# State times weights, formed per batch, ahead of the first layer: a cross-attention with a maxout FFN on one core

## The chip, the cores and the metric

The kernel runs on one core of a Trainium2 chip. The time is that of one execution on the device, in microseconds (us). The core has a matrix engine (TensorE, "PE" in the profile, with its weight loads as "PEld"), three engines for elementwise work (VectorE "DVE", ScalarE "ACT", GpSimd "POOL") and SyncE ("SP"), which here only issues transfers. Matmuls write to PSUM, a small memory of eight banks of 2 KB for each of 128 partitions; VectorE and ScalarE empty it into SBUF. Each engine takes its instructions in order and waits on semaphores for the others.

## The reference

There are 8 batches of 8 heads. Per head, 512 rows of x and 32 rows of state, 64 numbers each, read one another by attention. The results of all heads stand side by side as rows of 512, 544 per batch, 4352 in all, and go through a feed-forward layer with a maximum over three products.

```python
# x (8, 8, 512, 64), state (8, 8, 32, 64); w1, w2, w3 (512, 768); w_out (768, 512)
a      = softmax(x @ state^T / 8)        # 512 x 32 per head
xread  = a @ state                       # 512 x 64 per head
a2     = softmax(state @ x^T / 8)        # 32 x 512 per head
sread  = a2 @ x                          # 32 x 64 per head
X      = rows of [xread; sread], heads side by side       # 4352 x 512
h      = maximum(X @ w1, X @ w2, X @ w3)                  # 4352 x 768
out    = h @ w_out                                        # 4352 x 512, float32
```

## The kernel before

All inputs are loaded by GpSimd's queue, which turns float32 into bfloat16 on the way: the state (L65), eight transfers for a block-diagonal copy of it (bd_sb, L73), x in 32 transfers of 128 rows by all heads (x_sb, L85), the three weights (L90) and w_out (L93). The state's transposes go through PSUM and 64 small ScalarE copies into stateT_bd (L107, L109), where two heads stand in diagonal blocks.

Attention runs over the batches, and in each over four chunks of 128 rows. A chunk is transposed head pair by head pair (pxt, by the helper at L48), copied by ScalarE (xT, L139), multiplied with stateT_bd (ps, L143) and exponentiated (e_b, L151). VectorE sums over the 32 states (den, L157), takes the reciprocal (L160) and multiplies (a_sb, L162); a_sb is transposed (pat, L48) and copied (aT_b, L176). Then, for each of four head pairs, one matmul on 64 rows of the array forms xread, transposed (pxr, L184), which ScalarE copies into AT (L191); eight matmuls form sread and the column sums (psr, L195, L203), and VectorE divides (L211, L212, L216). pxr and psr have one PSUM buffer each.

AT holds all 4352 rows, transposed, in 4 x 128 partitions. The feed-forward stage runs over tiles of 512 rows, eight and a half of them. For each of six blocks m of 128 columns of h there are three times four matmuls of 512 columns (pw, L240); ScalarE copies the first product (L249), VectorE takes the two maxima (L250, L251) into ht. Six times four matmuls form the output of a tile (po, L256), ScalarE copies (L264) and SP stores (L265).

The order on each engine is made by a scheduler that fills free engines with what is ready; that is why transposes of the next chunk stand between the matmuls of the last one. The two stages open their own PSUM pools, so that only a little of the feed-forward runs before attention ends.

Of the kernel before, what the change touches and what calls it, by code (L numbers as in the profile page):

```python
# [15 lines left out]
def kernel(  # L17
# [9 lines left out]
):  # L27
    nc = tc.nc
# [7 lines left out]
    assert HD == d_model  # L36
    assert out.shape[0] == T and out.shape[1] == d_model

    NSC = S // 128
    NKT = HD // 128  # L40
    NMT = d_ff // 128
    NKO = d_ff // 128
    NHP = H // 2

    scale = 1.0 / (D ** 0.5)

    def tr(out_ap, in_ap, ident_ap, *, start, stop, tile_position=(0, 0)):
        nc.tensor.matmul(out_ap, in_ap, ident_ap,  # L48
                         is_transpose=True, start=start, stop=stop,
                         tile_position=tile_position)  # L50

    const = ctx.enter_context(tc.tile_pool(name="const", bufs=1))
    ident = const.tile([128, 128], BF16)
    make_identity(nc, ident)
    ones128 = const.tile([128, 128], BF16)
    nc.gpsimd.memset(ones128, 1.0)

    inpool = ctx.enter_context(tc.tile_pool(name="in", bufs=1))
    atpool = ctx.enter_context(tc.tile_pool(name="at", bufs=1))
    wpool = ctx.enter_context(tc.tile_pool(name="weights", bufs=1))  # L60

    AT = atpool.tile([128, NKT, T], BF16)

    state_sb = inpool.tile([32, B, H, D], BF16)
    nc.gpsimd.dma_start(out=state_sb, in_=state.rearrange("b h n d -> n b h d"))  # L65

    bd_sb = inpool.tile([128, B, 2, 128], BF16)
    nc.gpsimd.memset(bd_sb, 0.0)
    for hq in range(2):
        for hp4 in range(4):  # L70
            h = hq * 4 + hp4
            c0 = (h % 2) * 64
            nc.gpsimd.dma_start(  # L73
                out=bd_sb[hp4 * 32:(hp4 + 1) * 32, :, hq, c0:c0 + 64],
                in_=state[:, h, :, :].rearrange("b n d -> n b d"),
            )

    stateT_bd = inpool.tile([128, B, NHP, 2 * Ns], BF16)
    nc.gpsimd.memset(stateT_bd, 0.0)

    x_sb = inpool.tile([128, B, NSC, H, D], BF16)
    xr = x.rearrange("b h (sc p) d -> p b sc h d", p=128)
    for b in range(B):
        for sc in range(NSC):
            nc.gpsimd.dma_start(out=x_sb[:, b, sc, :, :], in_=xr[:, b, sc, :, :])  # L85

    w_sb = []
    for i, w in enumerate([moe_w1, moe_w2, moe_w3]):
        wt = wpool.tile([128, NKT, d_ff], BF16, name=f"w{i}")
        nc.gpsimd.dma_start(out=wt, in_=w.rearrange("(kk p) f -> p kk f", p=128))  # L90
        w_sb.append(wt)
    wout_sb = wpool.tile([128, NKO, d_model], BF16, name="wout")
    nc.gpsimd.dma_start(out=wout_sb,  # L93
                        in_=moe_w_out.rearrange("(kk p) f -> p kk f", p=128))

    with tc.tile_pool(name="psum_st", bufs=2, space=bass.MemoryType.PSUM) as pst:
        for b in range(B):
            pt = pst.tile([128, NHP, Ns], BF16)
            for hp in range(NHP):
                tr(  # L100
                    pt[:, hp, :],
                    state_sb[:, b, 2 * hp:2 * hp + 2, :],
                    ident[:Ns, :Ns],
                    start=(hp == 0), stop=(hp == NHP - 1),
                )
            for hp in range(NHP):
                nc.scalar.copy(out=stateT_bd[0:64, b, hp, 0:Ns],  # L107
                               in_=pt[0:64, hp, :])
                nc.scalar.copy(out=stateT_bd[64:128, b, hp, Ns:2 * Ns],  # L109
                               in_=pt[64:128, hp, :])  # L110

    xTpool = ctx.enter_context(tc.tile_pool(name="xT", bufs=3))
    epool = ctx.enter_context(tc.tile_pool(name="e", bufs=2))
    apool = ctx.enter_context(tc.tile_pool(name="a", bufs=3))
    aTpool = ctx.enter_context(tc.tile_pool(name="aT", bufs=2))
    redpool = ctx.enter_context(tc.tile_pool(name="red", bufs=6))

    with (
        tc.tile_pool(name="p_xT", bufs=2, space=bass.MemoryType.PSUM) as p_xT,
        tc.tile_pool(name="p_S", bufs=2, space=bass.MemoryType.PSUM) as p_S,  # L120
        tc.tile_pool(name="p_aT", bufs=2, space=bass.MemoryType.PSUM) as p_aT,
        tc.tile_pool(name="p_xr", bufs=1, space=bass.MemoryType.PSUM) as p_xr,
        tc.tile_pool(name="p_sr", bufs=1, space=bass.MemoryType.PSUM) as p_sr,
    ):
        for b in range(B):
            e_b = epool.tile([128, NSC, H, Ns], BF16, tag="e")
            aT_b = aTpool.tile([128, 2, NSC, 128], BF16, tag="aT")

            for sc in range(NSC):
                pxt = p_xT.tile([128, NKT, 128], BF16, tag="pxt")  # L130
                for hp in range(NHP):
                    tr(
                        pxt[:, hp, :],
                        x_sb[:, b, sc, 2 * hp:2 * hp + 2, :],
                        ident,
                        start=(hp == 0), stop=(hp == NHP - 1),
                    )
                xT = xTpool.tile([128, NKT, 128], BF16, tag="xT")
                nc.scalar.copy(out=xT, in_=pxt)  # L139

                ps = p_S.tile([128, NHP, 2 * Ns], F32, tag="pS")
                for hp in range(NHP):
                    nc.tensor.matmul(  # L143
                        ps[:, hp, :],
                        xT[:, hp, :],
                        stateT_bd[:, b, hp, :],
                        start=(hp == 0), stop=(hp == NHP - 1),
                        tile_position=(0, 0),
                    )

                nc.scalar.activation(  # L151
                    out=e_b[:, sc, :, :],
                    in_=ps.rearrange("p hp (q n) -> p hp q n", q=2),
                    func=AF.Exp, scale=scale,
                )
                den = redpool.tile([128, H], F32, tag="den")
                nc.vector.reduce_sum(out=den, in_=e_b[:, sc, :, :], axis=AX.X)  # L157
                rden = redpool.tile([128, H], BF16, tag="rden")
                with nc.allow_low_precision("softmax denom reciprocal"):
                    nc.vector.reciprocal(out=rden, in_=den)  # L160
                a_sb = apool.tile([128, H, Ns], BF16, tag="a")
                nc.vector.tensor_mul(  # L162
                    out=a_sb,
                    in0=e_b[:, sc, :, :],
                    in1=rden.unsqueeze(2).to_broadcast((128, H, Ns)),
                )

                pat = p_aT.tile([128, 2, 128], BF16, tag="pat")
                for hqq in range(2):
                    tr(  # L170
                        pat[:, hqq, :],
                        a_sb[:, 4 * hqq:4 * hqq + 4, :],
                        ident,
                        start=(hqq == 0), stop=(hqq == 1),
                    )
                nc.vector.tensor_copy(out=aT_b[:, :, sc, :], in_=pat)  # L176

            for hp in range(NHP):
                h0 = 2 * hp
                hq = h0 // 4  # L180
                p0 = (h0 % 4) * 32

                pxr = p_xr.tile([128, S], F32, tag="pxr")
                nc.tensor.matmul(  # L184
                    pxr,
                    bd_sb[p0:p0 + 64, b, hq, :],
                    aT_b[p0:p0 + 64, hq, :, :],
                    start=True, stop=True,
                    tile_position=(p0, 0),
                )  # L190
                nc.scalar.copy(out=AT[:, hp, b * SP:b * SP + S], in_=pxr)  # L191

                psr = p_sr.tile([128, 2, 2 * Ns], F32, tag="psr")
                for sc in range(NSC):
                    nc.tensor.matmul(  # L195
                        psr[:, 0, :],
                        x_sb[:, b, sc, h0:h0 + 2, :],
                        e_b[:, sc, h0:h0 + 2, :],
                        start=(sc == 0), stop=False,
                        tile_position=(0, 0),  # L200
                    )
                for sc in range(NSC):
                    nc.tensor.matmul(  # L203
                        psr[:, 1, :],
                        ones128,
                        e_b[:, sc, h0:h0 + 2, :],
                        start=False, stop=(sc == NSC - 1),
                        tile_position=(0, 0),
                    )
# [87 lines left out]
```

## Time and profile before

| | |
|---|---|
| runs | 278.49, 281.87, 282.01 us; median 281.87 us |
| profiled execution, first to last instruction | 279.6 us |
| mean granted TensorE clock in it | 0.896 of full |
| TensorE, first layer (L240) | 648 matmuls, 135.7 us busy |
| TensorE, second layer (L256) | 204 matmuls, 45.5 us busy |
| ScalarE's copies into AT (L191) | 32, 18.7 us busy; idle 29.5 us before them, for pxr |
| data read and written in memory | 15.73 MB and 8.91 MB |

The list of runs gives no time of its own for the profiled execution; its span stands in its place. Busy times of matmuls overlap with one another, since the engine is pipelined: 648 matmuls of the first layer last 370 ns each on average in the profile but start some 210 ns apart. So for TensorE it is better to read starts, or the chain of waits, than sums of durations. The granted clock is a share of full speed; it has two values in this trace, 1.00 and 0.50.

### The profile page before, as it was taken

The numbers are of one execution on the slowest core, as the hardware profiler recorded it, in microseconds if no ns is written. First come the engines' busy times: TensorE is split into PE (matmuls) and PEld (weight loads), VectorE is DVE, ScalarE is ACT, GpSimd is POOL, SyncE is SP. The second block draws the span as 40 slices with busy tenths as digits, with TensorE's granted clock in tenths as the row PEclk, the third lists the DMA queues.
The fourth block names the chain that finished last, engine by engine and source line by source line (L and its number), as shares of the span: only waits on it lengthen the run. The fifth ranks groups of instructions, "written<-read, shape, count | busy, mean of one in ns | idle before, by whom it ended". The sixth has DMA issues, their size and how long they took to land.

```text
span 279.6 us, 3945 instructions
## 1 busy us (share of the span) xinstructions
PE 239.7 (86%) x1492; PEld 122.7 (44%) x1492; DVE 131.9 (47%) x332; ACT 108.2 (39%) x249; POOL 41.1 (15%) x54
## 2 busy tenths in 40 slices
PE   0128878778776699999999999999999999999993
PEld 0017546535432344444444444444444444444581
DVE  0007897777877664334235235235135145145160
ACT  0989965645553132222322331331331332322321
POOL 9999990000000000000000000000000000000000
PEclk9999995555555589999999999999999999999999
DMA  5999999910000000120120120110210210210211
GB/s 38 59 144 149 154 155 204 208 25 0 2 1 2 0 1 0 43 109 0 58 94 0 73 77 2 76 75 0 76 77 0 79 74 0 96 56 2 109 41 75
DMA packets 44801, 17.01 MB, mean 61 GB/s; under 512 B 38128, under 2 KB 40432, under 8 KB 44784
## 3 DMA queue, kind: packets, MB, share of 16 engines
q0 software_dynamic: 39888, 7.87, 33.1%
q1 hardware_dynamic: 4896, 8.92, 8.3%
q8 instruction: 11, 0.18, 0.3%
q14 instruction: 6, 0.05, 0.1%
HBM read 15.73 MB, written 8.91 MB: 88 GB/s over the span
## 4 chain that ended last, share of the span: by engine, by line
PE 77%; POOL 12%; ACT 5%; DVE 3%; DMA 1%; issue 1%; ACTq 0%; POOLq 0%
PE pw L240 48%; PE po L256 16%; POOL x_sb L85 8%; PE pxr L184 5%; ACT AT L191 3%; PE psr L195 2%; PE pxt L48 2%; POOL bd_sb L73 2%; PE psr L203 2%; DMA x_sb<-in_x_dram 1%; PE ps L143 1%; PE pat L48 1%; ACT e_b L151 1%; DVE rd L211 1%; DVE a_sb L162 1%
## 5 line engine op out<-in xcount | busy, mean ns | idle before, releaser
L240 PE MATMUL pw<-AT,w 128*128 128x512 bf16 (+1 forms) x648 | 135.7, 370 | 0.0
L240 PEld LDWEIGHTS <-w 128*128 128x128 bf16 x648 | 63.3, 98 | 69.3 <-issue 1.6
L250 DVE TENSOR_TENSOR tmpm<-tmpm,pw 128x512 f32<-128x512 f32 (+1 forms) x54 | 35.5, 657 | 96.4 <-PE pw L240 91.0
L249 ACT COPY tmpm<-pw 128x512 f32<-128x512 f32 (+1 forms) x54 | 30.3, 562 | 87.1 <-PE pw L240 87.1
L256 PE MATMUL po<-wout,ht 128*128 128x512 bf16 x204 | 45.5, 379 | 0.0
L251 DVE TENSOR_TENSOR ht<-tmpm,pw 128x512 bf16<-128x512 f32 (+1 forms) x54 | 35.5, 658 | 5.7
L264 ACT COPY o_sb<-po 128x512 f32<-128x512 f32 x34 | 19.9, 586 | 39.0 <-PE po L256 39.0
L256 PEld LDWEIGHTS <-ht 128*128 128x128 bf16 x204 | 20.0, 98 | 23.9 <-DVE ht L251 1.6
L191 ACT CAST AT<-pxr 128x512 bf16<-128x512 f32 x32 | 18.7, 585 | 29.5 <-PE pxr L184 29.5
L85 POOL DMA_DIRECT2D x_sb<-in_x_dram x32 | 28.0, 1022 | 0.0
L184 PE MATMUL pxr<-aT_b,bd_sb 64*128 64x512 bf16 x32 | 16.9, 528 | 8.6 <-ACT AT L191 8.1
L211 DVE RECIPROCAL rd<-psr 128x64 f32<-128x64 f32 x32 | 17.8, 555 | 12.7 <-PE psr L203 11.8
L157 DVE TENSOR_REDUCE den<-e_b 128x8 f32<-128x256 bf16 x32 | 12.6, 412 | 22.6 <-ACT e_b L151 22.4
L48 PE MATMUL pxt<-ident,x_sb 128*128 128x128 bf16 x128 | 19.0, 277 | 3.8 <-ACT stateT_bd L109 2.8
L139 ACT COPY xT<-pxt 128x512 bf16<-128x512 bf16 x32 | 18.2, 594 | 3.2 <-PE pxt L48 3.1
L195 PEld LDWEIGHTS <-x_sb 128*128 128x128 bf16 x128 | 8.3, 119 | 22.0 <-DVE den L157 8.9
L48 PE MATMUL pt<-ident,state_sb 32*128 32x32 bf16 x32 | 2.0, 183 | 15.4 <-ACT stateT_bd L109 9.2
L143 PE MATMUL ps<-stateT_bd,xT 128*128 128x64 bf16 x128 | 11.5, 228 | 3.9 <-ACT e_b L151 2.6
L48 PE MATMUL pat<-ident,a_sb 128*128 128x128 bf16 x64 | 12.1, 288 | 3.0 <-DVE a_sb L162 3.0
L48 PEld LDWEIGHTS <-x_sb 128*128 128x128 bf16 x128 | 11.9, 127 | 5.0 <-issue 4.9
L162 DVE TENSOR_TENSOR a_sb<-e_b,rden 128x256 bf16<-128x256 bf16 x32 | 13.4, 422 | 0.5
L195 PE MATMUL psr<-e_b,x_sb 128*128 128x64 bf16 x128 | 12.6, 229 | 1.0 <-DVE AT L216 0.9
(27 smaller groups left out, 102.2 us busy)
## 6 DMA issues: line engine op xcount, KB each, us to landing
out_dram<-o_sb SPq DMA_DIRECT2D x34, 256.0 KB, 2.0
x_sb<-in_x_dram POOLq DMA_DIRECT2D x32, 128.0 KB, 4.9
w<-in_moe_w_dram POOLq DMA_DIRECT2D x3, 768.0 KB, 12.4
wout<-in_moe_w_out_dram POOLq DMA_DIRECT2D x1, 768.0 KB, 18.7
state_sb<-in_state_dram POOLq DMA_DIRECT2D x1, 256.0 KB, 4.6
bd_sb<-in_state_dram POOLq DMA_DIRECT2D x8, 32.0 KB, 2.3
```

What stands on the lines that cost most here:

```text
L48: nc.tensor.matmul(out_ap, in_ap, ident_ap, is_transpose=True, start=start, stop=stop, tile_position=tile_position)
L85: nc.gpsimd.dma_start(out=x_sb[:, b, sc, :, :], in_=xr[:, b, sc, :, :])
L184: nc.tensor.matmul(pxr, bd_sb[p0:p0 + 64, b, hq, :], aT_b[p0:p0 + 64, hq, :, :], start=True, stop=True, tile_position=(p0, 0),)
L191: nc.scalar.copy(out=AT[:, hp, b * SP:b * SP + S], in_=pxr)
L195: nc.tensor.matmul(psr[:, 0, :], x_sb[:, b, sc, h0:h0 + 2, :], e_b[:, sc, h0:h0 + 2, :], start=(sc == 0), stop=False, tile_position=(0, 0),)
L211: nc.vector.reciprocal(out=rd, in_=psr[:, 1, :])
L240: nc.tensor.matmul(pw[i][:, :nn], w_sb[i][:, kk, m * 128:(m + 1) * 128], AT[:, kk, n0:n0 + nn], start=(kk == 0), stop=(kk == NKT - 1), til ...
L249: nc.scalar.copy(out=tmpm[:, :nn], in_=pw[0][:, :nn])
L250: nc.vector.tensor_max(tmpm2[:, :nn], tmpm[:, :nn], pw[1][:, :nn])
L251: nc.vector.tensor_max(ht[:, m, :nn], tmpm2[:, :nn], pw[2][:, :nn])
L256: nc.tensor.matmul(po, ht[:, kt, j * 128:(j + 1) * 128], wout_sb[:, kt, :], start=(kt == 0), stop=(kt == NKO - 1), tile_position=(0, 0),)
L264: nc.scalar.copy(out=o_sb, in_=po)
```

## The change

The kernel is written anew around one identity. xread is a times state, per head; the first layer multiplies it with w. So for one batch, xread @ [w1 w2 w3] = a @ G, where G is state @ [w1 w2 w3], head by head: 256 rows (8 heads x 32 states) by 2304 columns. G is formed per batch in six pieces (`g_piece`) of eight matmuls each, with 64 rows and 32 columns of the array in use by each, and copied to SBUF by ScalarE. The first layer then contracts over 256, in two steps instead of four, and xread is never formed. The rows of sread still go through the weights, all 256 together at the end (`s_maxout`).

Other parts change with it. x is loaded with four neighbouring rows per partition, in eight transfers; the weights come in halves by column. Work of attention is done for a whole batch at once: `xt_piece` (16 transposes, two VectorE copies), `score_piece` (16 matmuls, one exponential of 1024 columns, a sum, a reciprocal, and the product with it on GpSimd), `sread_piece` (32 matmuls of 32 columns and 8 of 128, each on half of the array's columns) and `at_piece` (8 transposes, one copy). The order on the engines is the order of the code. The loop over batches has six slots; in slot m block m of the first layer of batch b is followed by parts of other batches: the second layer of b - 1, attention of b + 2, G of b + 1. All of these parts take their PSUM from one pair of two-bank buffers (tag "two"); the first layer has the other four banks (tag "pw").

```diff
+    ctx.enter_context(tc.manual_schedule())
...
+    load_x(0)
+    load_w(0)
+    load_w(1)
+    load_x(1)
+    load_x(2)
+    nc.gpsimd.dma_start(out=wout_sb, in_=moe_w_out.rearrange("(kk p) f -> p kk f", p=128))
+    for b in range(3, B):
+        load_x(b)
...
+    for g in range(2):
+        pt = pp.tile([128, 2048], BF16, tag="two", name="pt")
+        for t in range(8):
+            nc.tensor.transpose(
+                pt[:, 128 * t:128 * t + 128],
+                st_sb[:, 8 * g + t].rearrange("p c d -> p (c d)"), ident)
...
+    def xt_piece(b):
...
+        pxt = pp.tile([128, H, 2, 128], BF16, tag="two", name="pxt")
...
+            nc.vector.tensor_copy(out=xT[b][:, 4 * g:4 * g + 4], in_=pxt[:, 4 * g:4 * g + 4])
+
+    def score_piece(b):
+        ps = pp.tile([128, J, H, Ns], F32, tag="two", name="ps")
...
+        nc.scalar.activation(out=e[b], in_=ps, func=AF.Exp, scale=scale)
...
+        nc.vector.reduce_sum(out=den, in_=e[b], axis=AX.X)
...
+        nc.vector.reciprocal(out=rden, in_=den)
...
+        nc.gpsimd.tensor_mul(
+            out=a[b].rearrange("p j h n -> p (j h) n"),
...
+    def sread_piece(b):
+        psr = pp.tile([128, 1024], F32, tag="two", name="psr")
+        for j in range(J):
+            for h in range(H):
+                r, hh = h % 2, h // 2
+                nc.tensor.matmul(
+                    psr[64 * r:64 * r + 64, hh * Ns:hh * Ns + Ns],
+                    x_sb[b][:, h, j, :], e[b][:, j, slot(h), :],
+                    start=(j == 0 and hh == 0), stop=(j == J - 1), skip_group_check=True,
+                    tile_position=(0, 64 * r))
...
+    def at_piece(b):
+        pat = pp.tile([128, 2048], BF16, tag="two", name="pat")
...
+        nc.vector.tensor_copy(out=aT[b].rearrange("p q t -> p (q t)"), in_=pat[:, 0:1024])
...
+    def g_piece(b, u):
...
+        c, k = divmod(u, 3)
+        pg = pp.tile([128, 2, 512], F32, tag="two", name="pg")
+        for hh in range(NHP):
+            for r in range(2):
+                h = 2 * hh + r
+                nc.tensor.matmul(
+                    pg[32 * hh:32 * hh + 32, r, 0:384],
+                    bd[64 * r:64 * r + 64, b, h, r, :],
+                    w_sb[c][64 * r:64 * r + 64, hh, k * 384:(k + 1) * 384],
+                    start=True, stop=True, tile_position=(64 * r, 32 * hh))
+        nc.scalar.copy(out=G[b][:, :, u * 384:(u + 1) * 384], in_=pg[:, :, 0:384])
...
+    def maxout(b, m, n, lhs, rhs, nk):
...
+        for i in range(3):
+            p = pp.tile([128, 512], F32, tag="pw", bufs=4, name=f"pw{i}")
+            for k in range(nk):
+                nc.tensor.matmul(p[:, 0:n], lhs(i, m, k), rhs(k), start=(k == 0), stop=(k == nk - 1))
...
+        nc.scalar.copy(out=t0[:, 0:n], in_=pw[0][:, 0:n])
+        nc.vector.tensor_max(t1[:, 0:n], t0[:, 0:n], pw[1][:, 0:n])
+        nc.vector.tensor_max(ht[b][:, m, :], t1[:, 0:n], pw[2][:, 0:n])
...
+    def ffn_out(b, jj):
+        po = pp.tile([128, 2, d_model], F32, tag="two", name="po")
...
+        o = work.tile([128, 2, d_model], F32, tag="osb", bufs=3, name="osb")
+        nc.scalar.copy(out=o, in_=po)
...
+    for f in attention(0):
+        f()
+    for u in range(NG):
+        g_piece(0, u)
+    for f in attention(1):
+        f()
+
     for b in range(B):
...
+        slots = [[] for _ in range(NM)]
+        if b > 0:
+            slots[1].append(lambda: ffn_out(b - 1, 0))
+            slots[3].append(lambda: ffn_out(b - 1, 1))
+        if b + 2 < B:
+            for f, m in zip(attention(b + 2), (0, 2, 4, 5)):
+                slots[m].append(f)
+        if b + 1 < B:
+            for u in range(NG):
+                slots[u].append(lambda u=u: g_piece(b + 1, u))
+        for m in range(NM):
+            x_maxout(b, m)
+            for f in slots[m]:
+                f()
+    for m in range(NM):
+        s_maxout(m)
+        if m in (1, 3):
+            ffn_out(B - 1, m // 2)
+    ffn_out("s", 0)
```

GpSimd's queue before, its end (x_sb is x, w and wout are the weights). Its last rows are loads, with nothing behind them.

```order
L85 DMA x_sb<-in_x_dram 128x8x64 [waits DMASW0_49]
L90 DMA w_122<-in_moe_w_dram 128x4x768 [waits DMASW1_49]
L90 DMA w_124<-in_moe_w_dram 128x4x768 [waits DMASW2_49]
L90 DMA w_126<-in_moe_w_dram 128x4x768 [waits DMASW3_49]
L93 DMA wout<-in_moe_w_out_dram 128x6x512 [waits DMASW4_49]
L292 UNCONDITIONAL_BRANCH
```

GpSimd's queue after, from the weights on (w_88 and w_89 are their halves, x_81 to x_87 batches 1 to 7, a the normalized scores). The wait in brackets names one of eight semaphores of the loads, taken in turn.

```order
L81 DMA w_88<-in_moe_w_dram 128x4x384 x3
L81 DMA w_89<-in_moe_w_dram 128x4x384 x2
L81 DMA w_89<-in_moe_w_dram 128x4x384 [waits DMASW0_49]
L71 DMA x_81<-in_x_dram 128x8x256 [waits DMASW1_49]
L71 DMA x_82<-in_x_dram 128x8x256 [waits DMASW2_49]
L91 DMA wout<-in_moe_w_out_dram 128x6x512 [waits DMASW3_49]
L71 DMA x_83<-in_x_dram 128x8x256 [waits DMASW4_49]
L71 DMA x_84<-in_x_dram 128x8x256 [waits DMASW5_49]
L71 DMA x_85<-in_x_dram 128x8x256 [waits DMASW6_49]
L71 DMA x_86<-in_x_dram 128x8x256 [waits DMASW7_49]
L71 DMA x_87<-in_x_dram 128x8x256 [waits DMASW0_49]
L147 TENSOR_TENSOR a<-e,rden 128x1024 [waits DVE_49,Activation_49] x8
```

The weights moved ahead of all but the first batch of x, and the eight products that make a, which VectorE computed before, stand behind the last load.

ScalarE's queue before, in the middle of attention (AT is the transposed xread, e_b the exponentials, xT the transposed x):

```order
L191 CAST AT<-pxr 128x512 x4
L151 ACTIVATE e_b<-ps 128x256 x3
L139 COPY xT<-pxt 128x512
L151 ACTIVATE e_b<-ps 128x256
L139 COPY xT<-pxt 128x512 x3
```

ScalarE's queue after, in the loop, slots 1 to 3 of batch 1 (t is the copy of the first product, osb the output, G the piece of state times weights):

```order
L216 CAST t_699<-pw_690 128x512
L241 COPY osb<-po 128x1024
L202 CAST G<-pg 128x2x384
L216 CAST t_739<-pw_730 128x512
L141 ACTIVATE e<-ps 128x1024
L202 CAST G<-pg 128x2x384
L216 CAST t_788<-pw_779 128x512
```

The copies into AT and of xT are gone from ScalarE; a copy of G follows each copy of a first product, and the exponential and the output copies stand between the two.

More of the change, by code (lines that the diff above doesn't have):

```diff
@@ L65 @@
[L65 to L72, printed above, removed]
+    data = ctx.enter_context(tc.tile_pool(name="data", bufs=1))
+    wpool = ctx.enter_context(tc.tile_pool(name="weights", bufs=1))
+    work = ctx.enter_context(tc.tile_pool(name="work", bufs=2))
+    pp = ctx.enter_context(tc.tile_pool(name="pp", bufs=2, space=bass.MemoryType.PSUM))
@@ L93 @@
[L93 to L209, printed above, removed]
-                rd = redpool.tile([128, 2 * Ns], F32, tag="rd")
-                nc.vector.reciprocal(out=rd, in_=psr[:, 1, :])
-                nc.vector.tensor_mul(
-                    out=AT[0:64, hp, b * SP + S:b * SP + SP],
-                    in0=psr[0:64, 0, 0:Ns], in1=rd[0:64, 0:Ns],
-                )
-                nc.vector.tensor_mul(
-                    out=AT[64:128, hp, b * SP + S:b * SP + SP],
-                    in0=psr[64:128, 0, Ns:2 * Ns], in1=rd[64:128, Ns:2 * Ns],
-                )
@@ L270 @@
+    for m in range(NM):
+        s_maxout(m)
+        if m in (1, 3):
+            ffn_out(B - 1, m // 2)
+    ffn_out("s", 0)
 _INS = ['x', 'state', 'moe_w1', 'moe_w2', 'moe_w3', 'moe_w_out']
```

187 lines of the change are left out of this document (112 added, 75 removed).

## The prediction

> **What bounds the kernel now.** I read the page first (busy shares, the slices with the granted clock), then the chain that ended last, then stretches of the span, then the order of time on TensorE, last the groups of each engine by shape.
>
> ```profile
> span 279.6 us, 3945 instructions
> PE 239.7 (86%) x1492; PEld 122.7 (44%) x1492; DVE 131.9 (47%) x332; ACT 108.2 (39%) x249; POOL 41.1 (15%) x54
> PEclk9999995555555589999999999999999999999999
> 101.05 13.60 PE pw L240 x63
> 119.83 15.54 PE pw L240 x72
> 135.37 5.18 PE po L256 x24
> 264.87 7.86 PE pw L240 x72
> 272.73 2.60 PE po L256 x12
> 275.36 0.58 ACT o_sb L264
> ```
>
> There are two stages. From 101.05 us on the chain is TensorE alone: 72 matmuls of 512 columns take 15.54 us, 215.8 ns each, at full clock, and the same holds for the second layer (24 in 5.18 us). That stage is 174.3 us long and has no gap. The 101 us ahead of it are attention, over half of them at half clock:
>
> ```profile
> 26.00:38.00 12.00, 10.36 (x145) 7.13 (x142) 10.57 (x41) 10.39 (x24) 12.00 (x15) 1.00 2.37 151
> 38.00:42.00 4.00, 2.37 (x27) 1.22 (x27) 3.52 (x14) 2.62 (x6) 3.78 (x5) 0.95 2.15 159
> 42.00:95.00 53.00, 39.38 (x365) 23.99 (x363) 40.89 (x152) 25.23 (x54) 0.00 (x0) 0.50 0.33 58
> 42.00:49.00 7.00, 5.83 (x64) 4.33 (x62) 5.24 (x19) 3.81 (x9) 0.00 (x0) 0.50 1.16 203
> 30.27 0.37 PE L184 MATMUL pxr<-aT_b,bd_sb 64*128 64x512 bf16 x1 [0.29 <-ACT AT L191]
> 30.58 0.29 PE L195 MATMUL psr<-e_b,x_sb 128*128 128x64 bf16 x4
> 30.70 0.28 PE L203 MATMUL psr<-e_b,ones 128*128 128x64 bf16 x4
> 30.82 0.28 PE L48 MATMUL pat<-ident,a_sb 128*128 128x128 bf16 x2
> 30.93 0.28 PE L143 MATMUL ps<-stateT_bd,xT 128*128 128x64 bf16 x4
> 40.54 0.37 PE L184 MATMUL pxr<-aT_b,bd_sb 64*128 64x512 bf16 x1 [0.67 <-ACT AT L191]
> 42.84 0.40 PE L195 MATMUL psr<-e_b,x_sb 128*128 128x64 bf16 x4
> 43.06 0.40 PE L203 MATMUL psr<-e_b,ones 128*128 128x64 bf16 x4
> ```
>
> The columns after the length of a stretch are busy time and instructions of TensorE, weight loads, VectorE, ScalarE and GpSimd, then granted clock, DMA share and GB/s (as written to SBUF). In the rows in order of time the reader is to see start against start, not durations, which overlap. At full clock four matmuls of 64 columns take 0.12 us, 30 ns each, weight load included; a transpose of 128 columns takes 55 ns (two from 30.82 to 30.93). At half clock the same four take 0.22 us. A matmul on 64 rows of the array (pxr) holds the next one off for 0.31 us where its 512 columns need 0.216: a change between parts of the array and the whole costs about 0.095 us. And the clock fell at 42 with TensorE 2.37 us busy in the 4 us before and no gap over 0.67 us.
>
> **The change, part by part.** The first layer's contraction goes from four steps to two. A batch then needs 36 matmuls of 512 columns, not 72, and saves 36 x 0.2158 = 7.77 us; eight batches save 62.2 us. The state rows' part (72 of 256 columns, 7.86 us) and the second layer (5.18 us a batch, 2.60 us for the state rows) stay.
>
> What it adds is G: 48 matmuls a batch, each 64 rows by 32 columns of the array with 384 columns streamed. No row of before shows two such matmuls side by side. Their own columns take 384/512 x 215.8 = 162 ns. If the eight of a piece ran one behind the other, a piece would take 8 x 0.162 = 1.30 us; if they overlap and only issue parts them, 0.162 + 7 x 0.030 = 0.37 us. Below the first nothing but 0.162 us itself is possible. I take 0.37: the eight positions are disjoint and fill the array exactly once, each pair of row halves writes two different banks, and the row nearest to a 32-column piece is the small matmuls' 30 ns. [...]
>
> Attention of a batch is now 16 + 8 + 8 instructions of 128 columns and 16 + 32 of 64 or 32 columns: 32 x 0.055 + 48 x 0.030 = 3.2 us at full clock. Each G piece and the state read (64-column halves) change the array's partition twice: 14 x 0.095 = 1.3 us a batch, bounded by 0. [...]
>
> A full batch of the loop is then, on TensorE: 60 x 0.2158 = 12.95, G 2.2, attention 3.2, changes 1.3: **19.65 us**. What else runs beside it has prices in these groups:
>
> ```profile
> L251 DVE TENSOR_TENSOR ht<-tmpm,pw 128x512 bf16<-128x512 f32 x48 | 33.0, 687 | 5.0
> L157 DVE TENSOR_REDUCE den<-e_b 128x8 f32<-128x256 bf16 x32 | 12.6, 412 | 22.6 <-ACT e_b L151 22.4
> L176 DVE COPY aT_b<-pat 128x256 bf16<-128x256 bf16 x32 | 8.0, 249 | 2.6 <-PE pat L48 2.2 <-PE ps L143 0.3
> L211 DVE RECIPROCAL rd<-psr 128x64 f32<-128x64 f32 x32 | 17.8, 555 | 12.7 <-PE psr L203 11.8
> L160 DVE RECIPROCAL rden<-den 128x8 bf16<-128x8 f32 x32 | 4.9, 173 | 0.3
> L249 ACT COPY tmpm<-pw 128x512 f32<-128x512 f32 x48 | 28.1, 585 | 82.5 <-PE pw L240 82.5
> L249 ACT COPY tmpm<-pw 128x256 f32<-128x256 f32 x6 | 2.2, 373 | 4.6 <-PE pw L240 4.6
> L151 ACT ACTIVATE e_b<-ps 128x256 bf16<-128x256 f32 x32 | 11.6, 390 | 1.5 <-PE ps L143 1.5
> L85 POOL DMA_DIRECT2D x_sb<-in_x_dram x32 | 28.0, 1022 | 0.0
> L68 POOL MEMSET bd_sb<- 128x2048 bf16 x1 | 1.8, 1828 | 0.0
> state_sb<-in_state_dram POOLq DMA_DIRECT2D x1, 256.0 KB, 4.6
> out_dram<-o_sb SPq DMA_DIRECT2D x34, 256.0 KB, 2.0
> ```
>
> ScalarE: from 373 and 585 ns a column costs 0.83 ns, so 768 columns take 0.80, 1024 take 1.01, the exponential of 1024 takes 0.39 + 768 x 0.83 ns = 1.03. A batch: 6 x 0.585 + 6 x 0.80 + 2 x 1.01 + 1.03 = 11.4 us. VectorE: 12 x 0.687, three copies of at most 4 x 0.249, a sum of at most 4 x 0.412, reciprocals of 0.34 and 0.99 (6.8 ns a column between 173 and 555), a product of 0.3: at most 14.5 us. Both are below 19.65, so TensorE covers them, and if that cover goes (G faster, no changes) VectorE is next at 14.5. Walking one batch through the two shared PSUM pairs, the only waits that I find are the transposes of a and of x, which need what VectorE empties behind ht: about 0.4 us a batch.
>
> What I cost at nothing: the block tables bd (state lands 4.6 us after its issue, then 16 transposes and four copies, all done by some 11 us, under the 18 us of weight loads; without that cover they would cost 4 us); the table load for the exponential, earlier now; the stores, 16 of 512 KB for 32 of 256 KB on SP, which wait for ScalarE's copies alone and come some 10 us apart with three buffers, against 2.0 us to land. On ScalarE the copy of the first layer now stands behind a G cast and at times an output copy; it comes up to 1.3 us late, VectorE's two maxima with it, and of TensorE only the third bank group of the next slot, which the fourth bank and the slot's other pieces cover.
>
> The loop: batch 0 has no second layer (14.5), batches 1 to 5 are full (98.3), batch 6 has no attention (16.2), batch 7 neither that nor G (13.0), then the state rows and the last second layers 7.86 + 5.18 + 2.60 = 15.6; waits 6 x 0.4. Sum **160 us**.
>
> The start: GpSimd issues 17 loads at about 1.02 us, and the product for a(0), moved from VectorE to GpSimd, is queued behind all of them; the last load waits until the load eight before it, the last third of w's second half, has landed. Up to there 3.15 MB are written; at 203 GB/s from 2.5 us on they land at 18 to 19.5 us (at the 151 GB/s of the smaller pieces, at 25). With an issue of 1.0 and the product the queue gives a(0) at 22.5. No product of GpSimd is in the trace: its memset does 1024 elements in 0.91 us, three streams of that would be 2.7; I take 2.0, nearer to the upper end since two inputs are read and one output written. Behind GpSimd's product waits TensorE itself, which is in order: a(0)'s transposes, then G(0), six pieces paced by ScalarE (0.80 plus a hand-over): 29.2 us. Attention of batch 1 then runs alone at half clock: 16 transposes 1.8, copy 1.0, scores 0.95, exponential 1.03, sum 1.65, reciprocal 0.34, product 2.0, transposes 0.9, hand-overs 0.7: the loop starts at **39.5 us**. It starts cold: 7 us at half speed cost 3.5. Behind the last matmul came 0.02 + 0.58 us and then 3.7 us of output before; with a copy of 1.01 and eight short stores I take 5.
>
> Sum: 39.5 + 3.5 + 160 + 5 = 208 us as a span. The median of the runs, 281.87, stands 2.3 us above this execution's span, so **210 us**.
>
> **The rivals.** *G runs one piece behind the other*: 0.93 us more on each of 42 pieces in the loop is 39 us, and 11 us more at the start, where 8 x 0.324 us exceed ScalarE's 0.80: 260 us. For it: no row shows overlap; against it: the disjoint positions. *TensorE, in order, waits for buffers*: all pieces beside the first layer's share two pairs of banks; half a microsecond at each of 42 slots would give 231 us. For it, VectorE has up to 14.5 us of work in 19.65; against it, my walk found 0.4 us. *The clock stays at half* (the slower one): the 42 to 95 us stretch, 39.38 of 53 us busy, stayed at 0.50 all through. If the loop did, it would take 160 us more, 370 in all; it decides from 77 us of full-clock work on that run cold (281.87 x 1.02 less 210). Against it: the first layer's dense matmuls brought the clock back at 100 us and kept it for 174 us, and in the loop they are 12.95 of 19.65 us. [...]
>
> **How the numbers follow.** The forecast's case has 0.66, serial G 0.20, buffer waits 0.08, half clock 0.06. The forecast's own range is 194 to 225: the switch costs at 0 (9 us), faster G (8 us) on one side, loads at 151 GB/s (5.5 us), the weight loads and a longer product on the other. Two in ten are left out with 194 to 260: about 0.05 below, 0.06 for the clock and the upper half of serial G above. A difference of 2% is about what a measurement of this kernel can tell from none. Faster by more than that: all but the clock and part of serial G whose pieces also wait for weights (up to 17 us more, then ScalarE's hand-overs): 0.90; within 2%: 0.04; slower: 0.06.
>
> **What would show it.** Eight starts of a G piece within about 0.4 us (right) or 1.3 (serial). First-layer matmuls 0.216 us apart from the fifth batch on at clock 1.00. The first of them at 37 to 46 us, behind a wait for GpSimd's product. In the steady batch TensorE's idle time under 1 us of some 20. What would make it wrong: starts of G 0.16 apart, a granted clock of 0.50 inside the loop, or waits for ScalarE or VectorE in every slot.

## The result, and the profile after

The changed kernel takes 214.55 us (median of five runs, 212.65 to 215.94), the one before 280.62 in the same comparison: a ratio of 0.761, with a 95% interval of 0.755 to 0.766. The forecast was 210, from 194 to 260. The profiled execution took 215.94 us, 1.8 more than its span of 214.1. Two of the five runs, the profiled one among them, are over 1.5% above the fastest and count as slow; the ratio rests on the other three, whose median, 213.17 us, is what the experiments below are compared with.

The page of the changed kernel, its span, busy shares and slices with the granted clock:

```profile
span 214.1 us, 3798 instructions
PE 168.2 (79%) x1581; PEld 87.9 (41%) x1604; DVE 109.2 (51%) x170; ACT 90.8 (42%) x131; POOL 30.3 (14%) x31
PEclk9999999999999999999999969999999999999995
```

TensorE is still the busiest engine, with 71.5 us less busy time, but its share fell from 86 to 79%. The mean granted clock rose from 0.896 to 0.981. A full batch of the loop, in order of time on TensorE, from the first slot of batch 2 to that of batch 3 (where a row counts five or eleven matmuls of one block, a record is missing from the trace):

```profile
78.99 1.47 PE L212 MATMUL pw<-aT,G 128*128 128x512 bf16 x6
80.30 0.61 PE L127 MATMUL pxt<-ident,x 128*128 128x128 bf16 x8
82.67 0.61 PE L127 MATMUL pxt<-ident,x 128*128 128x128 bf16 x8 [1.77 <-DVE xT L130]
83.21 0.36 PE L197 MATMUL pg<-w,bd 64*32 64x384 bf16 x8
83.73 1.24 PE L212 MATMUL pw<-aT,G 128*128 128x512 bf16 x5 [0.16 <-issue]
84.81 2.75 PE L238 MATMUL po<-wout,ht 128*128 128x512 bf16 x12
87.49 0.35 PE L197 MATMUL pg<-w,bd 64*32 64x384 bf16 x8
87.78 1.47 PE L212 MATMUL pw<-aT,G 128*128 128x512 bf16 x6
...
98.99 0.35 PE L197 MATMUL pg<-w,bd 64*32 64x384 bf16 x8 [0.33 <-DVE ats L171]
99.28 1.47 PE L212 MATMUL pw<-aT,G 128*128 128x512 bf16 x6
```

Start against start, 78.99 to 99.28, a batch takes 20.29 us. A piece of G, eight matmuls, lets the next matmul start 0.29 us after its own first start (87.49 to 87.78). The largest gap is in the middle of the sixteen transposes of x: eight, then a wait of 1.77 us for VectorE's copy (xT), then eight. VectorE, in order of time, shows why the copy is late (L217 and L218 are the two maxima):

```profile
80.55 0.68 DVE L217 TENSOR_TENSOR t<-t,pw 128x512 bf16<-128x512 bf16 x1
81.33 0.69 DVE L218 TENSOR_TENSOR ht<-t,pw 128x512 bf16<-128x512 bf16 x1
81.93 0.69 DVE L130 COPY xT<-pxt 128x1024 bf16<-128x1024 bf16 x1
```

The copy of the first half stands behind both maxima of the block that the same slot computes, and these stand behind the copy of the transposed a (aT, at 79.95 us); VectorE works through them with no gap over 0.1 us. The second half of the transposes waits for the copy, although that half goes to the other bank of the pair.

The start, on TensorE, and GpSimd's last load and first product:

```profile
25.54 1.03 PE L180 MATMUL pat<-ident,a 128*128 128x128 bf16 x8 [8.23 <-POOL a L147]
...
30.93 1.01 PE L127 MATMUL pxt<-ident,x 128*128 128x128 bf16 x8 [0.18 <-ACT G L202]
...
41.41 2.34 PE L212 MATMUL pw<-aT,G 128*128 128x512 bf16 x5 [0.22 <-issue]
...
46.78 2.63 PE L212 MATMUL pw<-aT,G 128*128 128x512 bf16 x6
49.63 1.47 PE L212 MATMUL pw<-aT,G 128*128 128x512 bf16 x6
```

```profile
22.67 0.87 POOL L71 DMA_DIRECT2D x<-in_x_dram  x1 [1.61 <-DMA w<-in_moe_w_dram]
23.56 1.92 POOL L147 TENSOR_TENSOR a<-e,rden 128x1024 bf16<-128x1024 bf16 x1
```

TensorE stood still for 8.23 us until GpSimd had issued its last load (which waited for the weights) and made a(0). The loop starts at 41.41, and six first-layer matmuls still take 2.63 us at 46.78 but 1.47 at 49.63: half clock for some 8 us. The page's clock row says 9 there, because the trace holds no change of the clock earlier than the one that ends this stretch; the spacing of the matmuls is what tells.

Two stretches of the loop, one full batch each, with busy time and instructions of each engine, then granted clock, DMA share and GB/s:

```profile
83.70:104.00 20.30, 17.93 (x185) 9.05 (x188) 12.47 (x20) 10.48 (x16) 1.91 (x1) 1.00 0.13 54
124.30:146.30 22.00, 19.59 (x186) 9.49 (x189) 12.48 (x20) 10.59 (x16) 1.91 (x1) 0.92 0.12 49
```

The second is the same work, 1.7 us longer: the clock fell to half for one stretch of 3.4 us, right behind a wait like the one above. TensorE there:

```profile
124.34 2.34 PE L212 MATMUL pw<-aT,G 128*128 128x512 bf16 x5 [0.20 <-issue]
126.48 3.35 PE L238 MATMUL po<-wout,ht 128*128 128x512 bf16 x12
```

The profile of the third experiment below, which took 209.02 us, has a mean granted clock of 0.982, close to the 0.981 here; in the profiles of the other experiments that keep G as small tiles the mean is 0.988 to 0.995.

### The profile page after: what moved, and what is told of

It reads as the page before. It is cut to its first block, busy times and chain, and to the rows that moved or that the text cites. A ratio compares the mean times of both kernels' runs of the same rounds, so it can differ in the third digit from the quotient of the medians.

```text
span 214.1 us, 3798 instructions
## 1 busy us (share of the span) xinstructions
PE 168.2 (79%) x1581; PEld 87.9 (41%) x1604; DVE 109.2 (51%) x170; ACT 90.8 (42%) x131; POOL 30.3 (14%) x31
## 3 DMA queue, kind: packets, MB, share of 16 engines
q1 hardware_dynamic: 2688, 8.91, 10.5%
## 4 chain that ended last, share of the span: by engine, by line
PE 50%; DVE 17%; ACT 9%; issue 8%; DMA 6%; POOL 5%; another core or an unknown queue 2%; DVEq 0%; ACTq 0%; POOLq 0%
PE pw L212 21%; PE po L238 20%; DVE t L217 6%; DMA w<-in_moe_w_dram 6%; DVE ht L218 4%; ACT G L202 4%; PE pg L197 3%; PE pxt L127 3%; ACT t L216 2%; DVE xT L130 2%; DVE rd L170 2%; POOL a L147 2%; PE ps L136 2%; ACT osb L241 2%
## 5 line engine op out<-in xcount | busy, mean ns | idle before, releaser
L212 PE MATMUL pw<-aT,G 128*128 128x512 bf16 x269 | 72.2, 395 | 2.7 <-issue 1.1
L217 DVE TENSOR_TENSOR t<-t,pw 128x512 bf16<-128x512 bf16 (+1 forms) x54 | 35.0, 648 | 56.1 <-ACT t L216 49.7
L202 ACT CAST G<-pg 128x768 bf16<-128x768 f32 x48 | 38.1, 801 | 46.0 <-PE pg L197 46.0
L212 PEld LDWEIGHTS <-G 128*128 128x128 bf16 x288 | 25.4, 100 | 34.9 <-issue 13.1
L218 DVE TENSOR_TENSOR ht<-t,pw 128x512 bf16<-128x512 bf16 (+1 forms) x54 | 35.5, 658 | 5.6
L241 ACT COPY osb<-po 128x1024 f32<-128x1024 f32 x17 | 17.2, 1012 | 45.8 <-PE po L238 42.9
L216 ACT CAST t<-pw 128x512 bf16<-128x512 f32 (+1 forms) x54 | 31.0, 574 | 9.9 <-PE pw L212 9.8
L147 POOL TENSOR_TENSOR a<-e,rden 128x1024 bf16<-128x1024 bf16 x8 | 15.3, 1912 | 118.7 <-DVE rden L145 118.7
L127 PE MATMUL pxt<-ident,x 128*128 128x128 bf16 x128 | 12.2, 252 | 13.0 <-DVE xT L130 11.1
L197 PE MATMUL pg<-w,bd 64*32 64x384 bf16 x384 | 18.3, 357 | 2.8 <-DVE ats L171 1.6
## 6 DMA issues: line engine op xcount, KB each, us to landing
w<-in_moe_w_dram POOLq DMA_DIRECT2D x6, 384.0 KB, 10.5
```

The source lines that it names most:

```text
L127: nc.tensor.transpose(pxt[:, h, jj, :], x_sb[b][:, h, 2 * jj:2 * jj + 2, :].rearrange("p j d -> p (j d)"), ident)
L147: nc.gpsimd.tensor_mul(out=a[b].rearrange("p j h n -> p (j h) n"), in0=e[b].rearrange("p j h n -> p (j h) n"), in1=rden.rearrange("p j h - ...
L197: nc.tensor.matmul(pg[32 * hh:32 * hh + 32, r, 0:384], bd[64 * r:64 * r + 64, b, h, r, :], w_sb[c][64 * r:64 * r + 64, hh, k * 384:(k + 1) ...
L202: nc.scalar.copy(out=G[b][:, :, u * 384:(u + 1) * 384], in_=pg[:, :, 0:384])
L212: nc.tensor.matmul(p[:, 0:n], lhs(i, m, k), rhs(k), start=(k == 0), stop=(k == nk - 1))
L216: nc.scalar.copy(out=t0[:, 0:n], in_=pw[0][:, 0:n])
```

## The experiments

Times are medians; the changed kernel's 213.17 us is from its own comparison, and the kernel before was measured again beside each group, at 280.6 to 281.3.

**The wait inside the transposes.** Both copies go behind all sixteen transposes.

```diff
+        for h in range(H):
+            for jj in range(2):
+                nc.tensor.transpose(
...
         for g in range(2):
-            for h in range(4 * g, 4 * g + 4):
-                for jj in range(2):
-                    nc.tensor.transpose(
...
             nc.vector.tensor_copy(out=xT[b][:, 4 * g:4 * g + 4], in_=pxt[:, 4 * g:4 * g + 4])
```

> Edit: in the piece that transposes x, both VectorE copies stand behind all sixteen transposes, not one between the two halves. Theory A (TensorE's 1.77 us wait in the middle of this piece, for the copy of the first half that stands in VectorE's queue behind the maxima of the slot before, is lost time): the wait goes in six batches; the second layer's piece two slots on then waits for the emptied buffer, at most 0.5 us of the 1.77; the start gains 0.8. About 206.5 us. Rival B (the work of VectorE sets the pace there, and the wait comes back in full at the next use of the buffer pair): 214 us, the same.

Measured: 202.05 us, ratio 0.720 (0.715 to 0.725). On TensorE, in order of time:

```profile
92.53 1.47 PE L212 MATMUL pw<-aT,G 128*128 128x512 bf16 x6
93.84 1.06 PE L126 MATMUL pxt<-ident,x 128*128 128x128 bf16 x16
94.82 0.36 PE L197 MATMUL pg<-w,bd 64*32 64x384 bf16 x8
95.34 1.24 PE L212 MATMUL pw<-aT,G 128*128 128x512 bf16 x5 [0.16 <-issue]
96.42 2.75 PE L238 MATMUL po<-wout,ht 128*128 128x512 bf16 x12
...
110.89 1.47 PE L212 MATMUL pw<-aT,G 128*128 128x512 bf16 x6
```

A batch takes 18.36 us (92.53 to 110.89), 1.93 less, and the second layer (po) does not wait for the emptied pair at all: 11.1 us gained where theory A had 8. A holds, and the part of the wait that it expected back did not come. Rival B is out.

The start did not get shorter (the loop begins at 41.70, against 41.41). Between the two profiled executions, 214.1 and 199.9 us, the five full batches without the fall of the clock give 9.6 us, that fall 1.7, and batch 0 another 3.3. Of these 3.3 only 0.8 are the wait: the half clock ended about 2 us into the loop here, not 8. So part of this difference is the clock's, and the 1.93 us a batch are the part that is the copy's.

**G without tile positions.** Eight matmuls a piece on the whole array, with zero-padded tables.

```diff
-                nc.tensor.matmul(
-                    pg[32 * hh:32 * hh + 32, r, 0:384],
-                    bd[64 * r:64 * r + 64, b, h, r, :],
-                    w_sb[c][64 * r:64 * r + 64, hh, k * 384:(k + 1) * 384],
-                    start=True, stop=True, tile_position=(64 * r, 32 * hh))
+                nc.tensor.matmul(
+                    pg[:, r, 0:384], gz[:, b, r, hh, :],
+                    w_sb[c][:, hh, k * 384:(k + 1) * 384],
+                    start=(hh == 0), stop=(hh == NHP - 1))
```

> Edit: G is formed without tile positions: eight matmuls of 384 columns per piece as before, but each on the whole array with a table padded with zeros, summed over four. Theory A (the eight small-tile matmuls of a piece overlap on the array, 0.38 us a piece with the changes of partition against 8 x 0.162 = 1.30 us one behind the other): 0.92 us more on 42 pieces in the loop is 38.5, and about 11 more at the start at half clock: 264 us. Rival B (TensorE waits enough in every slot that a longer G hides in the waits, so that overlap was worth little): under 235 us.

Measured: 253.84 us, ratio 0.903 (0.898 to 0.909): 40.7 us more than with tiles. TensorE at the start and in the loop:

```profile
26.47 9.25 PE L203 MATMUL pg<-w,gz 128*128 128x384 bf16 x48
35.56 0.61 PE L134 MATMUL pxt<-ident,x 128*128 128x128 bf16 x8
...
85.00 1.46 PE L203 MATMUL pg<-w,gz 128*128 128x384 bf16 x8
86.30 1.46 PE L217 MATMUL pw<-aT,G 128*128 128x512 bf16 x6
```

A piece now takes 1.30 us in the loop (85.00 to 86.30), eight times 0.162. So the overlap of the tiles is shown, and worth nearly its whole price. A was 10 us too high, most of it at the start: the loop begins at 44.93, only 3.5 us later than with tiles and not 11, since the clock rises while the 48 dense matmuls run (9.25 us, not 15.5, and the transposes behind take 0.61 us for eight, not 1.01). It did not rise in the tiled pieces of the changed kernel, which wait for ScalarE between. The gain did not last: over the attention of batch 1, from 35.6 to 44.9 us, the mean granted clock was 0.70.

**The place of a(0) in GpSimd's queue.** The loads of batches 3 to 7 go behind the first product.

```diff
-    for b in range(3, B):
-        load_x(b)
...
+    xt_piece(0)
+    score_piece(0)
+    for b in range(3, B):
+        load_x(b)
+    sread_piece(0)
+    at_piece(0)
```

> Edit: the loads of batches 3 to 7 are issued behind GpSimd's product for a(0), not ahead of it. Theory A (the 8.2 us in which TensorE waits for a(0) come from the place of the product in GpSimd's queue, behind loads that wait for the landing of loads eight earlier): a(0) is ready at about 19.4 us, not 25.5, G(0) follows, and batch 1 then waits for its x, which lands at about 25.5: the loop starts some 5.4 us earlier, 209 us. Rival B (the weights' landing, the last at about 22.6 us, sets the start of G's pieces, so the order in the queue matters little): 213 to 214 us.

Measured: 209.08 us, ratio 0.742 (0.736 to 0.749).

```profile
20.36 1.04 PE L177 MATMUL pat<-ident,a 128*128 128x128 bf16 x8 [2.22 <-POOL a L144]
...
36.24 2.34 PE L209 MATMUL pw<-aT,G 128*128 128x512 bf16 x5 [0.22 <-issue]
```

TensorE, again: the transposes of a(0) start 5.2 us sooner and the loop too. A holds, and rival B's 213 to 214 us are out.

**The product on VectorE instead**, for all batches, with the loads as in the change.

```diff
-        nc.gpsimd.tensor_mul(
+        nc.vector.tensor_mul(
```

> Edit: the product that makes a is computed by VectorE for all batches, as before the change; the loads' order is unchanged. Theory A (the queue, not the engine's speed, cost the time at the start; in the loop VectorE has room for 1.2 us more a batch): a(0) at about 18.7 us, a(1) 0.7 us sooner; the loop starts about 6 us earlier and keeps its 20.3 us a batch: 208.5 us. Rival B (VectorE is the engine that the loop's waits end on, so its 1.2 us more come on top in each of six batches): 208.5 + 7 = 215.5 us.

Measured: 208.22 us, ratio 0.741 (0.736 to 0.746). TensorE:

```profile
35.12 2.34 PE L212 MATMUL pw<-aT,G 128*128 128x512 bf16 x5 [0.22 <-DVE ats L171]
...
80.73 1.47 PE L212 MATMUL pw<-aT,G 128*128 128x512 bf16 x6
...
101.02 1.47 PE L212 MATMUL pw<-aT,G 128*128 128x512 bf16 x6
```

The loop starts 6.3 us sooner, and a batch still takes 20.29 us (80.73 to 101.02) with 1.2 us more on VectorE. A holds, and rival B is out. The total of VectorE's work is not what the loop's waits end on; the order in its queue is.

**The change without G.** xread is formed per batch and the first layer contracts over 512; order, loads and attention stay.

```diff
-               lambda k: aT[b][:, k, :], 2)
+               lambda k: AT[b][:, k, :], NHP)
...
+            nc.tensor.matmul(
+                px[:, c, :], bd2[p0:p0 + 64, 2 * b + q, :], aT[b][p0:p0 + 64, q, :],
+                start=True, stop=True, tile_position=(p0, 0))
+        nc.scalar.copy(out=AT[b][:, 2 * half:2 * half + 2, :], in_=px)
```

> Edit: the changed kernel without G. xread is formed per batch by four matmuls on 64 rows (two pieces in slots 2 and 4, a ScalarE copy of 1024 columns each), and the first layer contracts over 512 again, 72 matmuls a batch; order, loads and attention stay. Theory A (the smaller contraction and the interleaving each give their own part): a full batch is 96 x 0.2158 + 3.2 + 1.1 + waits of 2 = 27.0 us on TensorE; start 39.5, batches 21.8 + 5 x 27.0 + 21.8 + 20.7, end 15.6 + 5, cold start and handing over 5: 264 us, so the contraction is worth about 50 us and all else about 17. Rival B (G costs TensorE and ScalarE nearly what the contraction saves, and the interleaving made the gain): under 235 us.

Measured: 255.34 us, ratio 0.908 (0.905 to 0.912). Two like places one batch apart, on TensorE:

```profile
100.42 0.39 PE L201 MATMUL px<-aT,bd 64*128 64x512 bf16 x2
...
116.97 0.61 PE L134 MATMUL pxt<-ident,x 128*128 128x128 bf16 x8 [0.93 <-DVE xT L137]
...
125.75 0.39 PE L201 MATMUL px<-aT,bd 64*128 64x512 bf16 x2
```

A batch takes 25.33 us, 1.7 less than A had; 1.1 of that is the wait inside the transposes, which is 0.93 here, not 2. So G is worth 255.34 - 213.17 = 42 us in this order, and everything else (interleaving, whole-batch pieces, loads) about 26. B is out; A holds with both sizes off by 8 or 9 us. The 26 us are not divided by any run, and the clock is in them: the kernel before spent some 58 us (42 to 100) at half clock with TensorE busy for 44.4 us of it, and this run's mean granted clock is 0.991 where that kernel's was 0.896.

**Filled waits ahead of the loop.** Ten matmuls that nobody reads stand in the attention of batch 1.

```diff
-    for f in attention(1):
-        f()
...
+    xt_piece(1)
+    filler(1)
+    score_piece(1)
+    filler(3)
+    sread_piece(1)
+    filler(6)
+    at_piece(1)
```

> Edit: ten matmuls of 512 columns, whose results nobody reads, fill TensorE's waits in the attention of batch 1 (1, 3 and 6 of them); nothing else changes. Theory A (the loop's first 8 us run at half clock because TensorE idles in the 10 us before, and filled waits keep the clock up): the first matmuls of the loop stand 0.216 us apart, not 0.427, and about 3.5 to 4 us are gained: 210.5 us. Rival B (the clock does not come back in so short a stretch): the fillers cost 0 to 1 us, 214 to 215.5 us.

Measured: 211.76 us, ratio 0.755 (0.752 to 0.758).

```profile
38.46 1.24 PE L264 MATMUL fill<-x,ident 128*128 128x512 bf16 x5 [0.16 <-issue]
...
41.14 1.46 PE L212 MATMUL pw<-aT,G 128*128 128x512 bf16 x6
...
44.52 0.61 PE L127 MATMUL pxt<-ident,x 128*128 128x128 bf16 x8 [1.48 <-DVE xT L130]
```

The fillers run at full clock by 38.5 us, and the loop's first six matmuls take 1.46 us. So the clock can be brought back there, as A had it. The gain is smaller than its 3.5 to 4 us: 1.4 us between the medians, with intervals that overlap (0.752 to 0.758 against 0.755 to 0.766), so its size stays unclear. Between the profiled executions batch 0 is 2.3 us shorter. One thing that took part of it back is in the rows: the wait inside the transposes of batch 2 is now 1.48 us where it was 0.78, and VectorE's copy takes 0.69 us at either clock (in the changed kernel at 33.78 us, at half clock, as at 81.93).

**A start of its own.** On top of the first experiment: x of batch 1 ahead of the weights, both attentions ahead of G(0), their products on VectorE.

```diff
     load_x(0)
+    load_x(1)
     load_w(0)
     load_w(1)
-    load_x(1)
...
+    xt_piece(0)
+    score_piece(0)
+    xt_piece(1)
+    score_piece(1)
+    sread_piece(0)
+    at_piece(0)
+    sread_piece(1)
+    at_piece(1)
+    for u in range(NG):
+        g_piece(0, u)
```

> Edit: the copies of x behind all its transposes (as in e1_copies_last); x of batch 1 loaded ahead of the weights; attention of batches 0 and 1 both ahead of G(0), their products that make a on VectorE. Theory A (the start is then bound by the landing of the weights alone, 3.67 MB at 0.2 MB a us, the last at about 25.2 us): the loop starts at about 26.5 us, where it started at 41.7 in e1_copies_last, whose time was 202.05: 187 us. Rival B (x of batch 2, which now lands behind the weights, and the cold clock take part of it back in batch 0): 191 us or more.

Measured: 193.73 us, ratio 0.689 (0.687 to 0.691).

```profile
19.48 0.39 PE L136 MATMUL ps<-bd,xT 128*128 128x64 bf16 x4 [2.91 <-DVE xT L130]
...
26.11 1.04 PE L157 MATMUL psr<-e,x 128*64 128x32 bf16 x32 [2.82 <-DVE ats L171]
...
33.42 2.34 PE L212 MATMUL pw<-aT,G 128*128 128x512 bf16 x5 [0.33 <-issue]
```

The loop starts at 33.42, and 41.70 - 33.42 is the 8.3 us gained. A missed by 6.7 us. B's range held the time, but not for its reason, since batch 0 grew by only 0.5 us. Neither theory had the reason that the start is not 26.5: TensorE waits twice for VectorE, whose queue has the sum, reciprocal and product of batch 0 ahead of the copies of batch 1, and the state reads behind them. The last run tests that: ScalarE copies x of batch 1 and the transposed a of batch 0, and the state reads move into the loop.

```diff
-            nc.vector.tensor_copy(out=xT[b][:, 4 * g:4 * g + 4], in_=pxt[:, 4 * g:4 * g + 4])
+            (nc.scalar.copy if b == 1 else nc.vector.tensor_copy)(
+                out=xT[b][:, 4 * g:4 * g + 4], in_=pxt[:, 4 * g:4 * g + 4])
...
-    sread_piece(0)
     at_piece(0)
-    sread_piece(1)
-    at_piece(1)
     for u in range(NG):
         g_piece(0, u)
+    at_piece(1)
...
+        if b == 0:
+            slots[1].append(lambda: sread_piece(0))
+            slots[3].append(lambda: sread_piece(1))
```

> Edit on top of e7_start_anew: ScalarE, idle there, copies x of batch 1 and the transposed a of batch 0; the state reads of batches 0 and 1 (and VectorE's 1.24 us for each) move into slots 1 and 3 of batch 0, which hold no second layer; G(0) stands ahead of the transposes of a(1). Theory A (in e7 the start, 33.4 us instead of the 26.5 that the loads allow, hung on VectorE's queue: the sum, reciprocal and product of batch 0 ahead of the copies of batch 1, and the state reads behind them): the loop starts at about 27 us, some 6.4 us sooner, and batch 0 grows by about 1.5 us of state reads: 189 us. Rival B (the loads land later than 25 us, or the half clock stretches batch 0 as far as the start shrinks): 192 to 194 us.

Measured: 189.33 us, ratio 0.675 (0.671 to 0.678), the fastest of all.

```profile
24.12 0.52 PE L199 MATMUL pg<-w,bd 64*32 64x384 bf16 x8 [1.32 <-DMA w<-in_moe_w_dram]
25.46 0.52 PE L199 MATMUL pg<-w,bd 64*32 64x384 bf16 x8 [0.81 <-DMA w<-in_moe_w_dram]
...
27.16 2.32 PE L214 MATMUL pw<-aT,G 128*128 128x512 bf16 x5 [0.22 <-issue]
```

The last two pieces of G(0) now wait for the weights themselves, and the loop starts at 27.16, 6.3 us sooner; batch 0 grew by 1.5 us, as A had it. A holds, and what is left right ahead of the loop is the landing of the weights.

## Why the prediction was right, point by point

Of the 6 us between the forecast's span, 208, and the profiled one, 214.1, the start has 1.9, the end 1.9, the fall of the clock in the loop 1.7 and the loop's own sum 0.6.

**Start: 39.5 forecast, 41.4 measured.** The chain was the right one, link by link: the last load held by a landing, the product, TensorE behind it, G(0) at ScalarE's pace, batch 1 alone at half clock. The error is in the first link: the landing that the last load waits for came at about 22.6 us, not at 18 to 19.5, and a(0) was ready at 25.5, not 22.5. I had 203 GB/s from 2.5 us on; the first 10 us moved 94 (last column), and only from there on it was about 200:

```profile
0.00:10.00 10.00, 1.89 (x16) 1.62 (x16) 3.68 (x6) 3.01 (x4) 8.89 (x16) 1.00 0.95 94
```

G(0) and the transposes ahead of it gave back 1.3 us (5.4, not 6.7). The third and fourth experiments show that the product's place behind the loads is what cost the time. The product itself took 1.92 us, where I had 2.0 between bounds of 0.9 and 2.7.

**G: right in kind.** Eight matmuls and both changes of the array's partition take 0.29 us and some 0.09 before; I had 0.56, so G cost 1.1 us a batch less. With 0.095 us for each change, as forecast, the eight themselves take 0.19 us, little more than the 0.162 of one alone, where I had 0.37. The range's 8 us for a faster G rested on no row of before; the 0.38 us a piece measured, against 0.56, are 7.6 us less over 42 pieces. The second experiment shows the price of eight that do not overlap, 1.30 us, and with it what the 260 us rival would have cost: 253.8.

**The loop's waits: the step that was wrong.** I found "about 0.4 us a batch" by walking through the pairs of banks. The real figure is 2.1 us (1.77 and 0.33), and the large one is in a place that I had not looked at: inside a piece, between two copies out of one buffer. I had named the transposes of x and the work that VectorE has ahead of them, but had counted the sixteen as one block. G's error had the other sign, and so had the state reads, 17 ns each where I had 30 (0.4 us a batch). The batch came out at 20.29 against 20.05, right by errors that cancel, which is luck; the first experiment shows that without the wait it is 18.36. The prediction's own sign for this, idle time of TensorE under 1 us in a batch, failed with 2.1.

**Cold start: 3.5 us.** The 7 us at half speed that it comes from were an estimate that no row of before shows. It fits the profiled execution, with some 8 us at half clock. But that length may be in part luck: it is about 2 us in the profile of the first experiment and about 4 in that of the third, with nearly the same work ahead of the loop, and filling the waits gave 1.4 us between the medians.

**End: 5 us.** It was 6.9, from the end of the last matmul at 207.2 to 214.1. The eight small stores are issued one behind the other, up to 211.9, and 2.2 us follow:

```profile
207.27 1.01 ACT L241 COPY osb<-po 128x1024 f32<-128x1024 f32 x1 [3.09 <-PE po L238]
...
208.31 3.63 SPq L245 DMA_DIRECT2D out_dram<-osb  x8
```

**The rivals.** Serial G did not happen. Waits for VectorE to empty a buffer happened in two places a batch, not at every slot, and over the loop cost about 9 us beyond the forecast's 2.4, where that rival had 21. The slower rival, half clock, came true in small: one stretch of 3.4 us in the profiled execution.

**Costed at nothing.** VectorE's 12.5 and ScalarE's 10.5 us a batch lie under TensorE's, as said, and 1.2 us more on VectorE changed nothing in the loop. That an engine is covered in sum says nothing of its order: both large waits of this kernel were for engines that are idle a third of the time or more (over the span VectorE was 51% busy, GpSimd 14%).

**Weight loads on column tiles.** The range holds a term for the weight loads of the 32 state reads, which no run shows. The rows on TensorE have, in its place:

```profile
95.61 0.68 PE L157 MATMUL psr<-e,x 128*64 128x32 bf16 x32
96.14 0.39 PE L164 MATMUL psr<-e,ones 128*64 128x128 bf16 x8
```

Thirty-two of them take 0.53 us from start to start, 17 ns each, loads included.

## What to carry to other kernels

When a contraction runs through a product with few rows (here 32 states a head), multiplying the weights with it first can halve the large product, here from 72 matmuls of 512 columns a batch to 36; small matmuls at disjoint tile positions then made the added one cheap, 0.29 us for eight against 1.30 on the whole array. In a hand-ordered kernel, look for each engine's queue position, not its load: here a load that waited held back the product behind it, and TensorE stood still for 8.23 us; a copy behind two maxima held back a transposition by 1.77 us inside a piece that looks like one block. Fill the sum of a start from the landing of the loads backwards, and ask of each engine what stands ahead of the one instruction that is waited for.

## What the runs showed of the hardware

The granted clock fell without an idle stretch as long as the fall: in the changed kernel it fell for 3.4 us behind waits of 0.33 and 1.77 us in a batch where TensorE was busy for 19.59 of 22.0 us. It did so in one of five nearly alike batches, and what decides between them no run shows. In the second experiment, where its mean from 35.6 to 44.9 us was 0.70, it fell at about 39 us behind waits of at most 1.11 us, with TensorE busy for about 2.4 of the 4 us from 35 to 39.

In the clock records of the two profiled executions, before and after, the stretches between two changes are 13.65, 58.03 and 180.91 us long in the kernel before and 75.09, 3.41 and 81.92 in the changed one: 4, 17, 53, 22, 1 and 24 times 3.413 us. So in these two the clock changed in steps of that length. The cold stretch of the loop was 2 us in the profile of the first experiment and 8 in that of the changed kernel; what sets its length no run shows.

The same G(0) brought the clock up in one form and not in the other: 48 whole-array matmuls ended at full clock within 9.25 us, and tiled pieces with waits for ScalarE between them, 4.4 us in all, stayed at half: eight transposes behind the first took 0.61 us, behind the second 1.01. Which is the cause, the tiles, the waits or the shorter time, was not tried apart.

Matmuls at eight positions of 64 rows by 32 columns start so close together that a piece of eight with 384 columns holds TensorE for 0.29 us, where one of 384 columns on the whole array takes 0.162 (the second experiment); and two column halves let 32 reads of 32 columns pass at 17 ns each, below the 30 ns that the smallest whole-array matmuls, of 64 columns, showed before. The eight of 128 columns behind them take 0.32 us with the change of partition, 40 ns each, where 128 columns on the whole array take 55.
